# An SSM attention, a gated FFN and a second FFN on one core: a new prologue, attention visits in two parts, and new ranks

## The chip, the cores and the metric

The kernel runs on one core of a Trainium2 chip. The metric is the device time of one execution in microseconds, as the median of several runs. The core's engines run side by side, each through its own list of instructions in order: TensorE (PE, matmuls; PEld its weight loads), VectorE (DVE), ScalarE (ACT), GpSimd (POOL) and SyncE (SP), whose queue issues nearly all transfers. They wait for each other by semaphores.

## What is computed

Three stages, the output of one being the input of the next:

```python
# 1: for each of 4 x 8 heads, in chunks of the sequence (S = 768, D = 32, N = 16)
cum = np.cumsum(np.log(np.clip(a, 1e-06, 1.0))[chunk], axis=-1)
L = np.exp(cum[:, :, :, None] - cum[:, :, None, :]) * causal
y = einsum(C B^T * L, x) + einsum(C, state) * exp(cum)
state = exp(cum[last]) * state + einsum(B, x) * exp(cum[last] - cum)
# 2: FFN with a token shift, on y as [4 * 768, 256]
xk = mu_k * x + (1 - mu_k) * x_prev;  xr = mu_r * x + (1 - mu_r) * x_prev
k = np.maximum(xk @ w_k, 0.0);  v = k * k @ w_v             # 256 -> 1024 -> 256
x = v / (1.0 + np.exp(-(xr @ w_r)))
# 3: FFN, 256 -> 2048 -> 256
h = x @ w_in;  out = (h - np.tanh(h)) @ w_out
```

The weights come in float64 and are decoded on the core into a high and a low part; each FFN product is made of three matmuls (high by high, low weight by high, high weight by low).

## The kernel before

*Attention.* Time is cut into 12 groups of 256 tokens (`GT`), three for each of four batches; a group holds 8 heads and four chunks of 64 (`NC4`, `L`). For group k: `xb_load` and `bc_load` fetch the inputs; `rows` fetches the cumulated logarithms in a high and a low part (`sr`, `rr`) from `dcum`, a scratch in DRAM that the prologue writes; `decays` makes the differences of them on PE (`pd`), `decays_exp` their exponential on ACT (`L`); `scores` makes C B^T (`pcb`), `mask` multiplies it into `L` on DVE. `prep_rows` and `scales_sum`/`scales_exp` make exp(cum) for a batch (`pc`, `er`), `group_scale` multiplies it into C (`cp`), `weigh` multiplies B by its decay (`bp`), `chain` carries the state (`st`).

A *visit* k on PE is `scores(k+1)`, `inter(k)` (C by state), `terms(k+1)` (what group k+1 adds to the state) and `intra(k)` (masked scores by x), 32 + 32 + 16 + 32 small fp32 matmuls (fewer `inter` or `terms` at the ends of a batch). `group_out` copies the result into `xall`.

*First FFN*: 6 blocks of 512 tokens. `mix` and `mix_ahead` make the two inputs; they are split into `xh` and `xl`; then 8 products `up`, 2 `receptance`, and 8 `down_part`, of six 512-column matmuls each (`MM6`); between up and down a relu, a square and the split into `h` and `l`, on ACT or DVE; `final` ends a block. *Second FFN*: 6 blocks of 16 products up and 16 down, with a polynomial on ACT and DVE between.

*Weights*: `decode` fetches a block of 512 KB (`raw`) and works on it with one square on ACT and five operations on DVE (`wd`, `keep`, the low part `w..l`), the high part on either.

*Order.* The start is written out by hand: `START` names pieces of the prologue, and each engine gets its instructions in that order. `warm` is 14 matmuls on a tile of zeros. After it, `Plan.run` orders everything: a task has the engines that can run it, a time for each, what it comes after, ring buffers that it takes and uses, and a rank. At each step the planner takes the task that can start first by its own model of times, the lower rank first among those. `RANK_...` are constants that set the ranks, so a change of them moves instructions on all engines.

```python
START = """
    xl qz Da Dla Dca Db0 Dx0 mr warm ms rc sc mk seg cA lA cC cD lC lD hA rA f00 f01 tA xe las cum tri heads zk r1 Db1 Dx1 W f10 f11 pr0 Db2 Dnk Dnr
    p0 dec dexp d0 e0 ps pe w0 ob u0 d1 e1 w1 m0 h0 s0 r2 v0 o0 nu
""".split()
```

`hA` and `rA` are the first cumulated sums for groups 0 and 1 in `sr`, `tA` the same for `kl`; `f00`, `f01`, `f10`, `f11` copy rows of `sr` into `rr` by DMA (`first_rows`); `rc`, `sc`, `heads` write constants with `affine_select` on POOL; `cum` makes the sums of all groups and writes `dcum`; `W` fetches the first weight block; `p0` to `v0` are group 0 up to its visit.

Of the kernel before, what the change touches and what calls it, by code (L numbers as in the profile page):

```python
# [11 lines left out]
I32 = mybir.dt.int32  # L12
# [28 lines left out]
SPARE = 3.89  # L41
RANK_T = 9.83
RANK_F0, RANK_F, RANK_R, RANK_U, RANK_D = 28.81, 25.83, 10.39, 7.47, 14.62
RANK_G0, RANK_G, RANK_LAG = 313.17, 0.0, -1.88
RANK_W0, RANK_W = -2.86, 5.66
RANK_X0, RANK_X = -69.94, 9.75
RANK_E0, RANK_E = 64.82, 8.06
# [12 lines left out]
    xl qz Da Dla Dca Db0 Dx0 mr warm ms rc sc mk seg cA lA cC cD lC lD hA rA f00 f01 tA xe las cum tri heads zk r1 Db1 Dx1 W f10 f11 pr0 Db2 Dnk Dnr  # L60
    p0 dec dexp d0 e0 ps pe w0 ob u0 d1 e1 w1 m0 h0 s0 r2 v0 o0 nu
# [4 lines left out]
START_AT = dict(P=12.5, A=10.8, V=11.2, G=8.0, S=10.0)  # L66
# [40 lines left out]
class Plan:  # L107
# [3 lines left out]
    OVERLAP = dict(P=0.0, A=0.09, V=0.08, G=0.04, S=0.0)  # L111
    SEEN = dict(P=0.22, A=0.05, V=0.05, G=0.05, S=0.0)
# [82 lines left out]
def chain_kernel(ctx, tc, xb, a, an, a0, bc, mu_k, mu_r, w_k, w_v, w_r, w_in, w_out, out):  # L195
# [38 lines left out]
    dec = const.tile([P, NG, NC4, NQ], F32, name="dec")  # L234
# [38 lines left out]
    for _ in range(NE):  # L273
# [5 lines left out]
        pair=Ring(3, ("pd", 1), ("pcb", 1), ("py", 0)), xb=Ring(3, 0, 1), bc=Ring(3, 0, 1, 2), rows=Ring(3, 0, 1), L=Ring(2, 0, 1), bp=Ring(2, 0, 1), cp=Ring(2, 0),  # L279
# [82 lines left out]
    CUM, LOW, ROW, NR, TN = 64, 96, 112, 116, 72  # L362
    CQ = NC4 * NQ
    kls = [att.tile([TN, S], F32R, name=f"kl{i}") for i in range(2)]
    heads = att.tile([TN, 2, NQ, NS], F32R, name="heads")
    sr = att.tile([NR, 3, 2, L], F32R, name="sr")
    rr = att.tile([NR, 3, CQ, L], F32R, name="rr")
    dcum = dram.tile([2, NG, CQ, 2, L], F32, name="dcum")
# [13 lines left out]
    def apart(k):  # L382
        return bct[k][:, GT:].rearrange("p (c e i) -> p c e i", c=NC4, e=2)
# [15 lines left out]
    def scales_sum(b, lo=0, hi=S):  # L399

        if b not in er:
            er[b] = att.tile([P, S], F32, tag="er", bufs=2, name="er")
        pcv = pcs[b] = bank("pc").rearrange("p a b -> p (a b)")
        for o in range(lo, hi, BLK):
            e = min(hi, o + BLK)
            PE.matmul(pcv[:, o - lo:e - lo], heads.rearrange("p h q n -> p (h q n)"), kls[b % 2][:, o:e], start=True, stop=True)
# [33 lines left out]
    def weigh(k):  # L440
# [3 lines left out]
            in1=dec[:, k].unsqueeze(3).to_broadcast([P, NC4, NQ, NS]), op=ALU.mult,  # L444
# [99 lines left out]
    def prologue(fetch1):  # L544
# [5 lines left out]
        ad = t2[:LOW + CQ, 0, 0:GT]  # L550
# [532 lines left out]
```

## Time and profile before

| | |
|---|---|
| median of 3 runs | 526.59 us (525.16 to 528.76) |
| profiled execution | 527.53 us, of it 525.8 us span |
| PE busy | 484.5 us (92%) |
| DVE busy | 402.9 us (77%) |
| ACT busy | 289.5 us (55%) |
| POOL busy | 8.8 us (2%) |
| mean granted TensorE clock | 0.958 |
| DMA, mean | 52 GB/s |

The span runs from the first to the last instruction in the profile. An engine's busy time is the union of its instructions; what it waited for is in the views of waits. The granted clock is a share of full speed, 2.4 GHz; 0.50 is 1.2 GHz.

### The profile page before, as it was taken

The page shows a single profiled execution, that of the slowest core. Times are in us where ns is not written, and L with a number is a line of the kernel's source. Part 1 is how long each engine was busy: PE and PEld are TensorE (multiplying, and loading weights), DVE is VectorE, ACT ScalarE, POOL GpSimd, SP SyncE. Part 2 cuts the span into 40 slices and gives each one's busy share as a digit, 9 for nine tenths or more (in the row PEclk, how much of TensorE's full clock was granted, in tenths as well). Part 3 has the DMA queues.
Part 4 walks back from the last instruction along what each step waited for, and adds up shares of the span by engine and source line. Part 5 has one row for each costly group of instructions (what it writes and reads, how often), then busy time and mean ns, then how long its engine had stood idle before and what let it go on. Part 6 is the DMA issues. An engine that isn't in the chain of part 4 may idle for free.

```text
span 525.8 us, 10261 instructions
## 1 busy us (share of the span) xinstructions
PE 484.5 (92%) x4448; PEld 386.1 (73%) x4448; DVE 402.9 (77%) x511; ACT 289.5 (55%) x368; POOL 8.8 (2%) x19
## 2 busy tenths in 40 slices
PE   6557897989999999999999999999999999999994
PEld 3335676867787888777778878888878888887883
DVE  5487887777876899999787787687776966887682
ACT  3265684538383677665756455455554554465551
POOL 6000000000000000000000000000000000000000
PEclk8585999889999999999999999999999999999998
DMA  2766423233100323321000010010010001001001
GB/s 89 222 163 179 159 87 138 61 105 100 38 2 2 104 72 90 94 81 43 0 1 0 0 41 0 1 40 2 1 41 0 1 0 41 0 0 41 0 1 46
DMA packets 15403, 27.47 MB, mean 52 GB/s; under 512 B 3368, under 2 KB 4472, under 8 KB 15352
## 3 DMA queue, kind: packets, MB, share of 16 engines
q1 hardware_dynamic: 15352, 26.75, 16.4%
q8 instruction: 37, 0.61, 0.5%
q14 instruction: 14, 0.11, 0.1%
HBM read 23.37 MB, written 3.34 MB: 51 GB/s over the span
## 4 chain that ended last, share of the span: by engine, by line
PE 70%; DVE 11%; ACT 6%; DMA 6%; issue 4%; POOL 1%; SPq 1%; POOLq 0%; ACTq 0%; DVEq 0%
PE acc L743 10%; PE acc L745 10%; PE acc L744 10%; PE ph L733 8%; PE ph L736 8%; PE ph L734 8%; PE pk L733 3%; PE pk L734 3%; PE pk L736 3%; PE pcb L471 2%; PE py L503 2%; PE py L481 1%; DMA raw<-in_w_out 1%; DMA rr<-sr 1%; ACT h L351 1%
## 5 line engine op out<-in xcount | busy, mean ns | idle before, releaser
L862 ACT ACTIVATE s<-ph 128x1024 f32<-128x1024 f32 (+1 forms) x49 | 49.4, 1009 | 71.9 <-PE ph L736 71.9
L867 DVE SCALAR_TENSOR_TENSOR f<-f,s 128x1024 f32<-128x1024 f32 (+1 forms) x49 | 58.8, 1200 | 33.9 <-ACT f L863 33.6
L351 ACT ACTIVATE h<-f 128x1024 fp32r<-128x1024 f32 (+1 forms) x47 | 48.9, 1041 | 49.7 <-DVE f L871 45.8
L733 PE MATMUL ph<-xh,winh 128*128 128x512 f32 x192 | 75.6, 394 | 0.0
L734 PE MATMUL ph<-xh,winl 128*128 128x512 f32 x192 | 75.6, 394 | 0.0
L743 PE MATMUL acc<-h,wouth 128*128 128x512 f32 x188 | 74.5, 396 | 0.2
L745 PE MATMUL acc<-l,wouth 128*128 128x512 f32 x188 | 74.3, 395 | 0.1
L744 PE MATMUL acc<-h,woutl 128*128 128x512 f32 x188 | 73.9, 393 | 0.0
L880 DVE TENSOR_TENSOR l<-f,h 128x1024 fp32r<-128x1024 f32 (+1 forms) x49 | 58.9, 1201 | 18.6 <-ACT h L351 18.0
L871 DVE TENSOR_TENSOR f<-ph,f 128x1024 f32<-128x1024 f32 (+1 forms) x49 | 58.8, 1200 | 3.3
L736 PE MATMUL ph<-xl,winh 128*128 128x512 f32 x192 | 60.0, 394 | 0.0
L863 ACT ACTIVATE f<-s,biases 128x1024 f32<-128x1024 f32 (+1 forms) x49 | 55.6, 1135 | 1.6
L743 PEld LDWEIGHTS acc<-h,wouth 128*128 128x128 f32 x188 | 35.4, 188 | 9.6 <-ACT f L863 1.4
L734 PEld LDWEIGHTS ph<-xh,winl 128*128 128x128 f32 x192 | 36.2, 188 | 8.3
L736 PEld LDWEIGHTS ph<-xl,winh 128*128 128x128 f32 x192 | 36.1, 188 | 8.2
L733 PEld LDWEIGHTS ph<-xh,winh 128*128 128x128 f32 x192 | 36.1, 188 | 8.2
L745 PEld LDWEIGHTS acc<-l,wouth 128*128 128x128 f32 x188 | 35.4, 188 | 9.2 <-DVE l L880 0.9
L744 PEld LDWEIGHTS acc<-h,woutl 128*128 128x128 f32 x188 | 35.5, 189 | 8.0
L733 PE MATMUL pk<-xh,wkh 128*128 128x512 f32 x96 | 40.1, 418 | 0.8 <-DVE st L538 0.8
L734 PE MATMUL pk<-xh,wkl 128*128 128x512 f32 x96 | 39.1, 408 | 0.0
L743 PE MATMUL acc<-h,wvh 128*128 128x512 f32 x96 | 38.5, 401 | 0.2 <-DVE xall L795 0.2
L745 PE MATMUL acc<-l,wvh 128*128 128x512 f32 x96 | 38.0, 395 | 0.5 <-DVE l L766 0.5
(134 smaller groups left out, 753.8 us busy)
## 6 DMA issues: line engine op xcount, KB each, us to landing
bct<-in_bc SPq DMA_DIRECT2D x12, 384.0 KB
xbt<-in_xb SPq DMA_DIRECT2D x12, 384.0 KB
raw<-in_w_in SPq DMA_DIRECT2D x8, 512.0 KB
raw<-in_w_out SPq DMA_DIRECT2D x8, 512.0 KB
out<-ob SPq DMA_DIRECT2D x11, 256.0 KB
raw<-in_w_k SPq DMA_DIRECT2D x4, 512.0 KB
raw<-in_w_v SPq DMA_DIRECT2D x4, 512.0 KB
raw<-in_w_r SPq DMA_DIRECT2D x1, 512.0 KB
```

The costliest lines, as they stand in the source:

```text
L351: A.activation(out=out, in_=in_, func=AF.Copy)
L733: PE.matmul(o, wh[:, k, ms], hi[:, k], start=k == 0, stop=False)
L734: PE.matmul(o, wl[:, k, ms], hi[:, k], start=False, stop=False)
L736: PE.matmul(o, wh[:, k, ms], lo[:, k], start=False, stop=k == 1)
L743: PE.matmul(acc[:, c], wh[:, k, cs], h[:, e], start=first, stop=False, skip_group_check=True)
L744: PE.matmul(acc[:, c], wl[:, k, cs], h[:, e], start=False, stop=False, skip_group_check=True)
L745: PE.matmul(acc[:, c], wh[:, k, cs], l[:, e], start=False, stop=last, skip_group_check=True)
L862: A.activation(out=s, in_=phs[j, i][:, e], func=AF.Square, accum_out=sums[:, c:c + 1])
L863: A.activation(out=qs[j, i][:, e], in_=s, func=AF.Square, scale=PA, bias=pbias)
L867: V.scalar_tensor_tensor(out=q, in0=q, scalar=PG, in1=s, op0=ALU.add, op1=ALU.mult)
L871: V.tensor_tensor(out=q, in0=phs[j, i][:, e], in1=q, op=ALU.mult)
L880: V.tensor_tensor(out=l[:, e], in0=qs[j, i][:, e], in1=f(h[:, e]), op=ALU.subtract)
```

## The change

*Prologue.* The constants in `rr` are no longer made by selects on full tiles: POOL makes a small tile (`mk`, 64 + 16 columns) and DVE (group 0) and ACT (group 1) copy it with a broadcast into `rr`; `heads` likewise from 8 columns. High and low rows, which lay in separate bands of partitions, now lie in one band (`CUM` to `ROW`) and are made from one tile of 48 rows; two per-partition numbers (`sign`) choose the high or the low part. `first_rows` is one transfer per half of the heads instead of two; the one for group 0 is issued on ACT's queue. The loads of group 1 (`Db1`, `Dx1`) and the first weight block (`W`) are issued before the first sums. `rows` is two transfers instead of four, `prep_rows` one instead of two, in layouts that follow a new `dcum`; `sr` and `rr` have two buffers instead of three (`Ring(2, ...)`). `w1` stands behind `h0` and `s0`. `fa` and `fb` put 8 and 6 matmuls on zeros behind `u0` and behind visit 0. The first `er` is made from `sr`, not from `kl`.

*Visits.* `visit` is cut into `visit_a` (`scores`, `inter`) and `visit_b` (`terms`, `intra`). They are two tasks; between them stands a task of 1.5 us on a made-up engine X, which issues nothing. The mask of the next group comes after the first half, no longer after the whole visit.

*Layout.* Inside `L`, `cp` and the second part of `bct` the half (e) now stands ahead of the chunk (c); column counts don't change.

*Ranks.* All constants have new values.

```diff
-SPARE = 3.89
-RANK_T = 9.83
-RANK_F0, RANK_F, RANK_R, RANK_U, RANK_D = 28.81, 25.83, 10.39, 7.47, 14.62
-RANK_G0, RANK_G, RANK_LAG = 313.17, 0.0, -1.88
-RANK_W0, RANK_W = -2.86, 5.66
-RANK_X0, RANK_X = -69.94, 9.75
-RANK_E0, RANK_E = 64.82, 8.06
+SPARE = 18.01
+PAUSE = 1.5
+RANK_T = 8.09
+RANK_F0, RANK_F, RANK_R, RANK_U, RANK_D = 26.98, 22.7, 14.0, 7.19, 15.13
+RANK_G0, RANK_G, RANK_LAG = 188.07, 0.0, -5.09
+RANK_W0, RANK_W = 5.2, 6.85
+RANK_X0, RANK_X = 162.75, 0.58
+RANK_E0, RANK_E = 65.74, 11.53
...
-    xl qz Da Dla Dca Db0 Dx0 mr warm ms rc sc mk seg cA lA cC cD lC lD hA rA f00 f01 tA xe las cum tri heads zk r1 Db1 Dx1 W f10 f11 pr0 Db2 Dnk Dnr
-    p0 dec dexp d0 e0 ps pe w0 ob u0 d1 e1 w1 m0 h0 s0 r2 v0 o0 nu
+    mk pidx still xl qz Da Dla Db0 Dx0 Dca warm sign m0t m0b seg m1t cA lA cC lC Db1 Dx1 hA tri cD lD xe f0 W m1b f1 heads las cum spread zk pr0 Db2 Dnk Dnr
+    p0 dec dexp d0 e0 ps pe w0 ob u0 fa d1 e1 m0 h0 s0 w1 v0 fb o0 nu
...
     def rows(k):
-        for x, o in enumerate((CUM, LOW)):
-            nc.sync.dma_start(out=f(sr[o:o + CQ, k % 3]), in_=dcum[x, k])
-        for h2 in range(2):
-            o = ROW + 2 * h2
-            nc.sync.dma_start(out=f(rr[o:o + 2, k % 3]), in_=dcum[:, k, :, h2])
+        nc.sync.dma_start(out=f(sr[CUM:TOK, k % 2]), in_=dcum[k].rearrange("h x q c i -> (x q c) h i"))
+        nc.sync.dma_start(out=f(rr[ROW:NR, k % 2]), in_=dcum[k].rearrange("h x q c i -> (h x) (q c) i"))
 
     def prep_rows(b, lo=0):
-        for x in range(2):
-            d = dcum[x, NGB * b + lo // GT:NGB * (b + 1)].rearrange("g (c q) h i -> (q h) (g c) i", c=NC4)
-            nc.sync.dma_start(out=f(kls[b % 2][32 * x:32 * x + NH, lo:]), in_=d)
+        d = dcum[NGB * b + lo // GT:NGB * (b + 1)].rearrange("k h x q c i -> (h x q) k (c i)")
+        nc.sync.dma_start(out=f(kls[b % 2][TOK:ROW, lo:]), in_=d)
...
     def visit(k):
 
+        visit_a(k)
+        visit_b(k)
+
+    def visit_a(k):
         if k + 1 < NG:
             scores(k + 1)
         out_bank(k)
         inter(k)
+
+    def visit_b(k):
...
+        def t_mk():
+
+            G.memset(mk, 0.0)
+            select(mk[0:L, 0:L], [[1, L]], 0, -1, ALU.is_ge, -32768.0)
+            for x in range(2):
+                select(mk[CUM:TOK, L:], [[1, CQ]], CQ * x, -1, ALU.not_equal, -1.0)
+
+        def moving(k, top, e):
+            if top:
+                o, i = rr[0:L, k].rearrange("p q c i -> p (q c) i"), mk[0:L, 0:L].unsqueeze(1).to_broadcast([L, CQ, L])
+            else:
+                o, i = rr[CUM:ROW, k].rearrange("p q c i -> p (q c) i"), mk[CUM:ROW, L:].unsqueeze(2).to_broadcast([ROW - CUM, CQ, L])
+            return lambda: copy(e, o, i)
...
+            o = sr[CUM:ROW].rearrange("p k h j -> p (k h j)")
+            V.tensor_tensor_scan(out=ad, data0=seg[CUM:ROW], data1=ad, initial=0.0, op0=ALU.mult, op1=ALU.add)
+            V.tensor_copy(o, ad)
+            V.tensor_scalar(out=ad, in0=ad, scalar1=sign[CUM:ROW, 0:1], scalar2=None, op0=ALU.mult)
+            V.scalar_tensor_tensor(out=o, in0=f(o), scalar=sign[CUM:ROW, 1:2], in1=ad, op0=ALU.mult, op1=ALU.add)
+
+        def first_rows(k, e):
             def fn():
                 for h2 in range(2):
-                    r = ROW + 2 * h2 + x
-                    o = (CUM, LOW)[x]
-                    nc.sync.dma_start(out=f(rr[r:r + 1, k]), in_=f(sr[o:o + CQ, k, h2]))
+                    r = ROW + 2 * h2
+                    e.dma_start(out=f(rr[r:r + 2, k]), in_=f(sr[CUM:TOK, k, h2]))
...
-                rw = put(dict(S=1.3), lambda e, k=k: rows(k), [], at(k - 1.2), [(R["rows"], k)], dma=0.2)
+                rw = put(dict(S=0.9), lambda e, k=k: rows(k), [], at(k - 1.2), [(R["rows"], k)], dma=0.2)
...
-                uses = [(R["L"], j), (R["xb"], j), (R["cp"], j), (R["state"], j), (R["bp"], k), (R["xb"], k), (R["bc"], k)]
-                need = [MK[j], CH[j], GS[j], XL.get(j), XL.get(k), BL.get(k), BPt.get(k), D.get(k), PS.get(b) if k < NG else None]
-                visited = put(dict(P=2.3 if k < NG else 1.1), lambda e, j=j: visit(j), need, at(j), take, uses)
+                use_a = [(R["cp"], j), (R["state"], j), (R["bc"], k)]
+                use_b = [(R["pair"], ("py", j)), (R["L"], j), (R["xb"], j), (R["bp"], k), (R["xb"], k)]
+                first_half = put(dict(P=1.85 if k < NG else 0.85), lambda e, j=j: visit_a(j), [CH[j], GS[j], BL.get(k), D.get(k), PS.get(b) if k < NG else None, MK[j]], at(j), take, use_a)
+                pause = put(dict(X=PAUSE), lambda e: None, [first_half])
+                visited = put(dict(P=1.25 if k < NG else 0.75), lambda e, j=j: visit_b(j), [pause, XL.get(j), XL.get(k), BPt.get(k)], at(j), (), use_b)
...
-            MK[k] = put(dict(V=t_dve(1024)), lambda e, k=k: mask(k), [visited, E.get(k)], at(k), (), [(R["pair"], ("pcb", k)), (R["L"], k)])
+            MK[k] = put(dict(V=t_dve(1024)), lambda e, k=k: mask(k), [first_half, E.get(k)], at(k), (), [(R["pair"], ("pcb", k)), (R["L"], k)])
```

Three places, as the programs list them. SP at the start (`raw<-in_w_k` is `W`, `rr<-sr` are the first rows), before:

```order
L557 DMA s<-in_a 112x256
L557 DMA f<-in_a 128x192
L557 DMA f<-in_an 96x256
L380 DMA bct<-in_bc 128x768
L376 DMA xbt<-in_xb 128x768
L622 DMA rr<-sr 1x16x64 x4
L629 DMA dcum<-l 96x2x256
```

and in the changed kernel:

```order
L565 DMA s<-in_a 48x256
L565 DMA f<-in_a 128x192
L381 DMA bct<-in_bc 128x768
L377 DMA xbt<-in_xb 128x768
L565 DMA f<-in_an 96x256
L381 DMA bct<-in_bc 128x768
L377 DMA xbt<-in_xb 128x768
L303 DMA raw<-in_w_k 128x2x512
L645 DMA rr<-sr 2x16x64 x2
L653 DMA dcum<-l 24x4x256 x2
```

The loads of group 1 and the first weights now stand ahead of the rows and of `dcum`; before they stood behind both. DVE in group 0's turn of the prologue, from the decay weights `bp` on, before:

```order
L442 TENSOR_TENSOR bp<-xbt,dec 128x256 x2
L521 TENSOR_TENSOR L<-pcb,L 128x512 x2
L535 COPY st<-py 128x64
L538 SCALAR_TENSOR_TENSOR st<-st,er,py 128x64 x3
L418 TENSOR_TENSOR cp<-bct,er 128x512
```

and in the changed kernel:

```order
L443 TENSOR_TENSOR bp<-xbt,dec 128x256
L528 TENSOR_TENSOR L<-pcb,L 128x512 x2
L542 COPY st<-py 128x64
L545 SCALAR_TENSOR_TENSOR st<-st,er,py 128x64 x3
L419 TENSOR_TENSOR cp<-bct,er 128x512
L443 TENSOR_TENSOR bp<-xbt,dec 128x256
```

`weigh(1)`, the second `bp`, stood ahead of the mask and stands behind `cp`. PE in visit 5 (`pcb` scores, `py<-cp` inter, `py<-xbt,bp` terms, `py<-L` intra, `acc` a down product, `pc` the sums of a batch), before:

```order
L471 MATMUL pcb<-bct 32x128 x32
L481 MATMUL py<-cp,st 32x64 x32
L496 MATMUL py<-xbt,bp 32x64 x16
L503 MATMUL py<-L,xbt 32x64 x32
L733 MATMUL pk<-xh,wkh 128x512
```

and in the changed kernel:

```order
L472 MATMUL pcb<-bct 32x2x64 x32
L482 MATMUL py<-cp,st 32x64 x32
L765 MATMUL acc<-h,wvh 128x512
L766 MATMUL acc<-h,wvl 128x512
L767 MATMUL acc<-l,wvh 128x512
...
L407 MATMUL pc<-kl_109,heads 128x512
L407 MATMUL pc<-kl_109,heads 128x256
L497 MATMUL py<-xbt,bp 32x64 x16
L504 MATMUL py<-L,xbt 32x64 x32
```

A product of six matmuls (three of them shown) and the sums stand between `inter` and `terms`, where before nothing did.

## Rows read from the trace of the kernel before

**Rows 1.** Busy time by stage; mean clock, DMA share and GB/s at the end.

```profile
0.00:50.60 50.60, 30.01 (x776) 19.13 (x777) 32.23 (x73) 22.89 (x37) 8.85 (x19) 0.70 0.55 161
57.00:101.00 44.00, 37.35 (x761) 30.17 (x746) 35.19 (x59) 29.28 (x36) 0.00 (x0) 0.96 0.36 117
101.00:180.00 79.00, 73.64 (x1438) 59.85 (x1438) 60.47 (x89) 45.17 (x54) 0.00 (x0) 0.98 0.18 55
180.00:515.00 335.00, 333.89 (x1438) 269.31 (x1436) 268.33 (x279) 189.63 (x240) 0.00 (x0) 1.00 0.08 24
20.00:253.00 233.00, 209.11 (x3191) 167.61 (x3191) 194.01 (x302) 142.97 (x176) 0.12 (x1) 0.93 0.30 91
```

**Rows 2.** PE's waits from 50.6 to 180: us in total, times, longest.

```profile
PE py L503 <- issue: 9.3, 6, 3.2
PE py L496 <- issue: 1.2, 1, 1.2
PE py L481 <- ACT f L783: 1.0, 1, 1.0
...
```

**Rows 3.** Busy time and counts between the ends of two such waits.

```profile
76.68:91.71 15.03, 11.88 (x253) 9.72 (x254) 12.07 (x19) 7.07 (x9) 0.00 (x0) 1.00 0.38 126
111.33:127.33 16.00, 15.08 (x254) 11.96 (x254) 13.47 (x22) 7.35 (x7) 0.00 (x0) 0.89 0.28 87
```

**Rows 4.** The page: busy engines with instruction counts; a DMA queue.

```profile
PE 484.5 (92%) x4448; PEld 386.1 (73%) x4448; DVE 402.9 (77%) x511; ACT 289.5 (55%) x368; POOL 8.8 (2%) x19
...
q8 instruction: 37, 0.61, 0.5%
```

**Rows 5.** Busy time and clock (third from the end) after two long waits.

```profile
92.20:95.60 3.40, 3.40 (x14) 2.60 (x10) 2.36 (x6) 1.73 (x3) 0.00 (x0) 0.50 0.52 143
112.70:116.10 3.40, 3.40 (x10) 2.63 (x9) 3.29 (x8) 0.00 (x0) 0.00 (x0) 0.50 0.74 211
```

**Rows 6.** Timeline of the prologue: start, us, engine, line, operation [idle before].

```profile
1.09 6.04 PE L554 MATMUL acc<-quiet 128*128 128x512 bf16 x14 [1.09 <-DVE quiet L658]
...
12.31 1.22 PE L427 MATMUL pd<-rr,sr 116*128 116x512 f32 x2 [1.11 <-DMA rr<-sr]
...
13.95 2.42 SPq L622 DMA_DIRECT2D rr<-sr  x4
...
14.71 1.08 PE L496 MATMUL py<-xbt,bp 64*32 64x64 f32 x32 [0.96 <-ACT L L438]
...
18.52 0.42 DVE L442 TENSOR_TENSOR bp<-xbt,dec 128x256 f32<-128x256 f32 x1 [4.44 <-DMA xbt<-in_xb]
18.86 1.28 DVE L521 TENSOR_TENSOR L<-pcb,L 128x512 f32<-128x512 f32 x2
...
21.03 1.20 PE L427 MATMUL pd<-rr,sr 116*128 116x512 f32 x2 [5.24 <-DMA rr<-sr]
...
21.21 0.69 DVE L418 TENSOR_TENSOR cp<-bct,er 128x512 f32<-128x512 f32 x1
...
25.97 1.27 PE L503 MATMUL py<-L,xbt 64*32 64x64 f32 x59
```

**Rows 7.** Timeline of DVE from 28 us on, and PE's first FFN matmul.

```profile
28.94 1.23 DVE L538 SCALAR_TENSOR_TENSOR st<-st,er,py 128x64 f32<-128x64 f32 x4 [2.11 <-ACT er L409]
...
31.29 0.42 DVE L313 TENSOR_SCALAR wd<-raw 128x512 uint32<-128x512 uint32 x1
31.62 0.68 DVE L328 TENSOR_TENSOR wkl<-keep,wkh 128x512 fp32r<-128x512 f32 x1
32.23 0.68 DVE L316 SCALAR_TENSOR_TENSOR wd<-raw,wd 128x512 uint32<-128x512 uint32 x1
...
38.38 1.22 DVE L521 TENSOR_TENSOR L<-pcb,L 128x1024 f32<-128x1024 f32 x1
...
45.24 1.22 DVE L766 TENSOR_TENSOR xl<-f,xh 128x1024 fp32r<-128x1024 f32 x1
...
50.63 0.77 PE L733 MATMUL pk<-xh,wkh 128*128 128x512 f32 x1 [0.83 <-DVE st L538]
```

More of the change, by code (lines that the diff above doesn't have):

```diff
@@ L357, in select @@
         G.affine_select(out=t, in_=f(t), pattern=pattern, base=base, channel_multiplier=cm, compare_op=op, fill=fill)
-    CUM, LOW, ROW, NR, TN = 64, 96, 112, 116, 72
+    CUM, TOK, ROW, NR = 64, 96, 112, 116
     CQ = NC4 * NQ
[L364 to L368, printed above, removed]
+    kls = [att.tile([ROW, S], F32R, name=f"kl{i}") for i in range(2)]
+    heads = att.tile([NR, 2, NQ, NS], F32R, name="heads")
+    sr = att.tile([NR, 2, 2, L], F32R, name="sr")
+    rr = att.tile([NR, 2, NQ, NC4, L], F32R, name="rr")
+    dcum = dram.tile([NG, 2, 2, NQ, NC4, L], F32, name="dcum")
     NC = NB * NH * S // GT
@@ L403, in scales_sum @@
         pcv = pcs[b] = bank("pc").rearrange("p a b -> p (a b)")
+        hv = heads.rearrange("p h q n -> p (h q n)")
+        if hi == GT:
+            PE.matmul(pcv[:, 0:GT], hv, sr.rearrange("p k h j -> p (k h j)"), start=True, stop=True)
+            return
         for o in range(lo, hi, BLK):
             e = min(hi, o + BLK)
-            PE.matmul(pcv[:, o - lo:e - lo], heads.rearrange("p h q n -> p (h q n)"), kls[b % 2][:, o:e], start=True, stop=True)
+            PE.matmul(pcv[:, o - lo:e - lo], hv[0:ROW], kls[b % 2][:, o:e], start=True, stop=True)
     def scales_exp(b, lo=0, hi=S):
@@ L415, in group_scale @@
     def group_scale(k):
-        cp[k] = att.tile([P, NC4, 2, L], F32, tag="cp", bufs=2, name="cp")
-        by = scale(k).rearrange("p (c i) -> p c i", c=NC4).unsqueeze(2).to_broadcast([P, NC4, 2, L])
-        V.tensor_tensor(out=cp[k], in0=apart(k), in1=by, op=ALU.mult)
+        cp[k] = att.tile([P, 2, NC4 * L], F32, tag="cp", bufs=2, name="cp")
+        by = scale(k).unsqueeze(1).to_broadcast([P, 2, NC4 * L])
+        V.tensor_tensor(out=cp[k], in0=bct[k][:, GT:].rearrange("p (e t) -> p e t", e=2), in1=by, op=ALU.mult)
     pds = {}
@@ L423, in decays @@
         pd = pds[k] = bank("pd")
-        mt[k] = att.tile([P, 2, NC4, 2, L], F32, tag="L", bufs=2, name="L")
+        mt[k] = att.tile([P, 2, 2, NC4, L], F32, tag="L", bufs=2, name="L")
         for g in range(2):
-            by = rr[:, k % 3].rearrange("p (c q) i -> p c (q i)", c=NC4)[:, :, 2 * L * g:2 * L * (g + 1)]
-            PE.matmul(pd[:, g], sr[:, k % 3].rearrange("p h j -> p (h j)"), by, start=True, stop=True)
+            by = rr[:, k % 2, 2 * g:2 * g + 2].rearrange("p q c i -> p (q c i)")
+            PE.matmul(pd[:, g], sr[:, k % 2].rearrange("p h j -> p (h j)"), by, start=True, stop=True)
     def flat(k):
-        return mt[k].rearrange("p g c e i -> p g (c e i)")
+        return mt[k].rearrange("p g e c i -> p g (e c i)")
     def parts(split):
@@ L470, in scores @@
                     r = quarter(q)
-                    PE.matmul(pcb[quarter(2 * h2 + jh), hp, t], bct[k][r, o:o + 32], bct[k][r, GT:][:, t], start=c == 0, stop=c == NC4 - 1, skip_group_check=True)
+                    PE.matmul(pv[quarter(2 * h2 + jh), hp, :, c], bct[k][r, o:o + 32], apart(k)[r, :, c], start=c == 0, stop=c == NC4 - 1, skip_group_check=True)
     def out_bank(k):
@@ L628, in t_cum @@
             V.tensor_tensor(out=cf[:, 1], in0=ca, in1=f(cf[:, 0]), op=ALU.subtract)
-            nc.sync.dma_start(out=dcum.rearrange("x g c h i -> x (g c h i)").rearrange("x (p s) -> p x s", s=GT), in_=f(cf))
+            for x in range(2):
+                nc.sync.dma_start(out=dcum[:, :, x].rearrange("k h q c i -> (k h) q (c i)"), in_=f(cf[:, x]))
         def t_las():
@@ L649, in t_nu @@
             G.memset(xall[:, :, 0:NB * (S + 1)].rearrange("p c (b s) -> p c b s", b=NB)[..., 0:1], 0.0)
-        def more(k):
-            return lambda: A.activation(out=rr[:, k], in_=f(rr[:, 0]), func=AF.Copy)
         def dummy(func):
@@ L1053, in columns @@
         return np.ascontiguousarray(channels(v).reshape(2, P).T)
-    heads = a.reshape(NB, NQ, 2, NGB, NC4, L).transpose(0, 3, 4, 1, 2, 5)
-    sums = np.ascontiguousarray(heads).reshape(NG, NC4 * NQ, 2 * L)
-    two = sums[0:2].transpose(1, 0, 2).reshape(NC4 * NQ, 2 * P)
+    heads = a.reshape(NB, NQ, 2, NGB, NC4, L).transpose(0, 3, 2, 1, 4, 5)
+    two = heads[0, 0:2].transpose(2, 3, 0, 1, 4).reshape(NC4 * NQ, 2 * P)
+    one = heads[0, 0].reshape(2, NQ, GT)
     def f64(v):
@@ L1063 @@
         "xb": np.concatenate([tokens(x), tokens(B)], axis=3),
-        "a": np.ascontiguousarray(heads.transpose(4, 5, 0, 1, 2, 3)).reshape(P, NG * NC4 * NQ),
-        "an": sums.reshape(-1, GT),
-        "a0": np.concatenate([np.tile(a[0, :, 0:GT], (8, 1)), two, two, two]),
+        "a": np.ascontiguousarray(heads.transpose(2, 5, 0, 1, 3, 4)).reshape(P, NG * NC4 * NQ),
+        "an": np.ascontiguousarray(heads).reshape(-1, GT),
+        "a0": np.concatenate([two, two, one[0], one[0], one[1], one[1]]),
         "bc": np.concatenate([states(B), apart(C)], axis=2),
```

88 lines of the change are left out of this document (41 added, 47 removed).

## The prediction

> **What bounds the kernel now.** I read the busy time by stage first [rows 1]. From 180 to 515 us TensorE (PE) is busy 333.9 of 335 us at full clock: the second FFN and the last blocks of the first are bound by PE, and their matmuls don't change. The time that an edit can win lies ahead of that. In the first 50.6 us PE is busy for 30.0, at a mean granted clock of 0.70; from 57 to 101 it is idle for 6.7 us, from 101 to 180 for 5.4.
>
> Then I read what PE waited for after its first FFN matmul [rows 2]. Two entries of 9.3 and 1.2 us stand at the attention matmuls of `intra` and `terms` under "issue": seven waits, for which no semaphore is shown. Third, the count of PE instructions between the ends of such waits [rows 3]: 254 matmuls and 253 weight loads, then 253 and 254, the same 507 each time whatever FFN work lies between. The page has a DMA queue of the kind "instruction" with 37 packets and 0.61 MB [rows 4], 16.5 KB each; PE's 8,896 matmuls and weight loads over 37 make 240 for each, about half of 507. I read these waits as PE running out of its own instruction stream: the 112 matmuls of a visit are some 450 short instructions for 3 to 4 us, those of an FFN product of 1.38 us only 12.
>
> Fourth, the clock after the two longest waits [rows 5]: the one of 3.2 us is followed by 3.4 us at 0.50 of full speed, which is 1.2 GHz, and the one of 2.2 us before 111.35 by another 3.4.
>
> Last, the opening [rows 6]. The `rr<-sr` transfers for group 1 are issued at 13.95, after two group loads and a weight block, and `decays(1)` starts at 21.03, 5.24 us late. VectorE (DVE) stands 4.44 us before `weigh(1)`, whose data come in the same batch, and the mask of group 0, which stands behind it, starts at 18.86, though its exponential was done when it released `terms(0)` at 14.71.
>
> **The change part by part.** The sum is made against the profiled execution, 527.53 us with a span of 525.8; it lies 0.9 over the median of 526.59. I take three terms and a charge.
>
> *Term A, the opening.* Removed: the selects over 1024 columns on GpSimd, two memsets, one of two sets of row transfers. Added: two DVE copies of 1024 columns, five tiny DVE operations, four passes over 48x256, one ACT copy more, and a wait of the first `rr<-sr` on ACT behind the third logarithm and a table load. No row shows a spread copy from a small tile; it lies between an operation on 512 columns, 0.68, and the mask on 1024, 1.22 [rows 7]. Both are below the selects, but ACT's order now holds the transfer. I take `decays(0)`, and the exponential with it, to stay where they are, with bounds of 1.3 us earlier and 1.7 later (a copy of 1.22 more and half a microsecond of issue). Group 1 and the first weights are issued right at the start, so `decays(1)` and `weigh(1)` find their data; `weigh(1)` now stands behind the mask and the state chain.
>
> So from 14.7 on DVE takes mask, chain and `cp` in the 3.04 us that they took from 18.86 to 21.90 [rows 6], and is done near 17.7. On PE `terms(0)` ends at 15.8 and the eight new fills come next: at the 0.43 us of the warm-up matmuls [rows 6] 3.4 us, to 19.2. They lie beside the DVE work, except for 1.5 us. Then `decays(1)` to `intra(0)`: 6.2 us as from 21.03 to 27.24 at half the clock, or down to 3.1 at the full one. They end between 22.3 and 25.4 against 27.24; I take 23.5, since PE has no gap left between 12.3 and there. Six more fills cost 1.3 to 2.6 us. From the end of `intra(0)` to the state chain of group 1 it took 1.7 us, to 28.94 [rows 7]: now it starts near 23.5 + 1.3 + 1.7 = 26.5.
>
> From there DVE sets the pace up to `xl`, the last factor of the first FFN input. In the new order 23 rows stand from that chain to `xl`. In a packed stretch DVE starts the next operation 0.6 us after one on 512 columns (31.62 to 32.23), 0.33 after a short one and 1.2 after one on 1024 [rows 7]: 16.4 us in all. That gives 42.9 for the end of `xl`, which was at 46.46. The first four matmuls of a product don't need `xl`, so PE starts the first product near 42, where it started at 50.63, after visit 2 in both: 8.6 us. By then it will also have done `decays(4)`, `scores(4)` and `inter(3)`, 2.2 us of work that came later. Term A is 10.8 us; with all bounds against it 8, with all for it 13.
>
> *Term B, the visit in two parts.* `visit_b` is ranked apart, with a pause of 1.5 us that occupies no engine. In the new PE order the visits 3, 4 and 6 to 11 have two products between `inter` and what follows, 2.76 us; visit 5 has one and the sums' two matmuls, about 1.7, and visits 1 and 2 have only the sums. These products are work that PE had to do anyway, so they cost nothing where their inputs are ready; the cover is DVE and ACT being ahead with the mixes and squares. The six waits in `intra` lasted 0.76 to 3.16 and the one in `terms` 1.2 [rows 2]. With 2.76 us between, a wait of 3.16 leaves 0.4; with 1.7 it leaves up to 1.5. Of 10.5 I take 9.5; the bounds are 6 (half of the blocks end elsewhere in the visit, where nothing stands between) and 10.5.
>
> The Trainium skill, page "Runtime: NRT & Kernel Launch", section "Instruction fetch mechanics", says that an engine's instructions come in blocks of 16 KiB and that crossing into the next is "mostly hidden". The block size agrees with the 16.5 KB of [rows 4], the hiding does not agree with the 10.5 us. By that sentence the stall would have another cause, terms B and C would be nothing, and the gain 12.9 us smaller; this is the second rival.
>
> *Term C, the clock.* Two stretches of 3.4 us at 0.50 follow waits of 3.16 and 2.18 us [rows 5]. Half of each is lost, 1.7 us, 3.4 in all. Where no such wait is left, neither is the fall. The slow start of the first FFN (50.6 to 54.7, 2.0 us) I leave as it is, because PE is idle for half of the 10 us before it in the new order too. Bounds 0 and 5.4.
>
> *The charge, new waits.* The new ranks let four visits run before the first FFN block and put products where the planner's model has their inputs ready. Two places look tight to me: the first down product needs `l`, which stands 13 DVE rows or 10 us behind `xl`, while PE reaches it 9 us after its first product, some 2 us early; and the second `wv` block is due within 1 us of its use. I charge 4 us, with bounds of 0 (the largest wait on another engine between 50.6 and 180 was 1.0 [rows 2]) and 8.
>
> Row buffers go from three to two: `rows(k)` is issued after `decays(k-2)`, two visits earlier, and four issues become two. Cost nothing unless the transfer lands later than that; this is the third rival. Stacking halves and heads differently changes no column count of a matmul or of a DVE operation.
>
> Sum: 10.8 + 9.5 + 3.4 - 4 = 19.7. 527.5 - 19.7 = 507.8 for the profiled execution, and 0.9 less for the median: **507**. All bounds one way give 8 + 6 + 0 - 8 = 6, the other way 13 + 10.5 + 5.4 = 29.
>
> **The rivals.** *DVE becomes the bound.* Between 20 and 253 us DVE was busy for 194.0 [rows 1]. By the counts of the two orders it gives ACT copies worth 3.6 us, net: 190. With my forecast these have to fit in 213 us, 89%; it was 80% from 57 to 101 and 77% from 101 to 180 (35.19 of 44, 60.47 of 79). Where it can't be packed beyond 84%, the first FFN ends at 20 + 226 = 246, a gain of 7 to 8 us: 519. For: a long stretch where weights, masks and squares all wait for one engine. Against: much of DVE's idle time followed PE's own waits, and goes with them.
>
> *The split does nothing.* If the issue waits have another cause, or move to another place in the visit, terms B and C fall away: 10.8 - 4 = 6.8, 520. For: the pause is the planner's alone, PE isn't made to wait for anything. Against: the constant count of 507 [rows 3].
>
> *Slower, by the row buffers.* `decays(k)` stands ahead of `scores` on PE, in order, and its rows are queued on SyncE behind the group load and weight blocks. If they land late, all of PE waits: the worst seen is 5.24 us [rows 6]. At ten visits the gain of 19.7 is gone from 2 us a visit on, and at 3.5 us the time is 526.6 + 15 = 542. Against: after the third visit 10 us and more lie between one visit and the next, and in the trace no later `decays` waited for rows.
>
> **How the numbers follow.** Forecast (a gain of 13 to 28) 0.65; DVE bound 0.18; split without effect 0.09; slower 0.05; the rest, 0.03, a gain over 28. The range leaves out the slower case, the upper part of the two weak ones and the best end: 499 to 518. A measurement of this kernel can tell about 1%, 5.3 us, from no change. Faster by more: 0.65 + 0.03 and most of the two middle cases, 0.9. Within 1%: 0.05. Slower by more: 0.05.
>
> **What would show it.** The first FFN product near 42; `decays(1)` no longer waiting for `rr<-sr`; the mask of group 0 near 15. In the visits after it, "issue" at `intra` and `terms` under 2 us in total, and no fall of the clock between 60 and 180. New waits of PE on DVE `l` or `xl`, or on a weight, would be the charge; DVE busy for over 90% from 40 to 100 with PE waiting for it, the first rival. The end of the first FFN (the last `final`, before 253) should move to about 233, and the rest of the program should only shift. Wrong I would be above all if PE's new products stand and wait where the old order had work.

## The result, and the profile after

The changed kernel takes 505.6 us, median of 4 runs (505.0 to 507.4), against 526.9 before (4 runs, 525.2 to 528.8): a ratio of 0.960, 95% interval 0.956 to 0.964, 21.3 us. The profiled execution took 507.4 us, with a span of 505.7; it is the slowest of the four, with a mean clock of 0.978 where the others have 0.984 to 0.986, so the trace shows a little more half clock than they have.

The windows of the changed kernel, as those of [rows 1]; the columns are busy time with the number of instructions of PE, PEld, DVE, ACT, POOL, then the clock, the DMA share and GB/s:

```profile
0.00:20.00 20.00, 13.90 (x141) 6.48 (x149) 12.48 (x37) 8.13 (x15) 6.01 (x21) 0.83 0.60 184
20.00:42.80 22.80, 18.23 (x777) 13.55 (x761) 19.59 (x37) 15.71 (x24) 0.11 (x1) 0.85 0.72 219
42.80:100.00 57.20, 54.69 (x1138) 43.70 (x1128) 53.35 (x90) 43.06 (x54) 0.00 (x0) 0.97 0.45 138
100.00:180.00 80.00, 79.77 (x1075) 64.66 (x1074) 70.28 (x99) 53.76 (x64) 0.00 (x0) 1.00 0.18 53
180.00:505.70 325.70, 315.86 (x1361) 253.86 (x1360) 245.73 (x250) 172.45 (x219) 0.00 (x0) 0.99 0.06 20
20.00:230.00 210.00, 201.56 (x3190) 161.68 (x3175) 188.76 (x285) 144.15 (x180) 0.11 (x1) 0.98 0.32 97
```

From 42.8 to 180 us PE is now idle for 2.7 us in all. The last row is the answer to the first rival: DVE is busy for 188.8 of 210 us, 90%, and PE hardly waits for it. The waits of PE in that stretch, beside [rows 2]:

```profile
PE py L482 <- issue: 2.1, 1, 2.1
PE py L482 <- ACT f L805: 0.4, 1, 0.4
PE py L482 <- DVE f L807: 0.2, 1, 0.2
```

Seven issue waits of 10.5 us at `intra` and `terms` have become one of 2.1 us, at `inter` (L482 now). Ahead of 42.8 us there is another one, of 2.43 us, at `scores(3)` (33.82 in the timeline below); the prediction has no such wait. The opening in the timeline, beside [rows 6] and [rows 7] (start, duration, engine, line; in brackets the idle time before, and what ended it):

```profile
8.99 1.31 ACTq L645 DMA_DIRECT2D rr<-sr  x1
...
12.46 0.90 PE L428 MATMUL pd<-rr,sr 116*128 116x512 f32 x2 [2.60 <-DMA rr<-sr]
...
14.02 1.29 DVE L528 TENSOR_TENSOR L<-pcb,L 128x512 f32<-128x512 f32 x2 [0.95 <-ACT L L439]
...
15.54 3.59 PE L217 MATMUL acc<-quiet 128*128 128x512 bf16 x8
...
18.57 1.31 PE L428 MATMUL pd<-rr,sr 116*128 116x512 f32 x2
...
25.00 1.23 DVE L545 SCALAR_TENSOR_TENSOR st<-st,er,py 128x64 f32<-128x64 f32 x4 [0.34 <-ACT er L410]
...
33.82 0.47 PE L472 MATMUL pcb<-bct 32*32 32x128 f32 x8 [2.43 <-issue]
...
41.56 1.22 DVE L788 TENSOR_TENSOR xl<-f,xh 128x1024 fp32r<-128x1024 f32 x1
...
42.84 0.50 PE L755 MATMUL pk<-xh,wkh 128*128 128x512 f32 x1
...
230.06 1.22 DVE L817 TENSOR_TENSOR xall<-acc,s 128x1024 f32<-128x1024 f32 x1 [3.42 <-PE acc L767]
```

`decays(1)` starts at 18.57 with no wait for `rr<-sr`, the first FFN product at 42.84 instead of 50.63, and the last `final` at 230.06 instead of 252.06. Ahead of 180 us the clock stands at 0.50, which is 1.2 GHz, in three stretches: 12.8 to 19.6, and (windows as above)

```profile
74.20:77.60 3.40, 3.40 (x10) 2.62 (x9) 3.40 (x7) 1.58 (x2) 0.00 (x0) 0.51 0.83 266
33.30:40.10 6.80, 6.23 (x190) 4.69 (x190) 5.42 (x9) 6.80 (x11) 0.00 (x0) 0.50 0.79 251
```

The first of these follows the issue wait that ended at 73.60; the second sets in during the one that ended at 33.82. Before, such stretches made 41.0 us in all, now 17.0.

The span is PE's busy time plus its idle time, so the 20.1 us can be booked without a remainder: idle time fell from 41.3 to 23.2 us (7.9 less ahead of 45 us, 6.2 less from 45 to 100, 5.1 less from 100 to 180, and 1.1 more after 180), busy time from 484.5 to 482.5, in spite of 14 fills.

### The profile page after: what moved, and what is told of

Read it like the earlier page. It is cut to its first block, busy times and chain, and to the rows that moved or that the text cites. A ratio compares the mean times of both kernels' runs of the same rounds, so it can differ in the third digit from the quotient of the medians.

```text
span 505.7 us, 10270 instructions
## 1 busy us (share of the span) xinstructions
PE 482.5 (95%) x4462; PEld 382.3 (76%) x4462; DVE 401.4 (79%) x509; ACT 293.1 (58%) x374; POOL 6.1 (1%) x22
## 4 chain that ended last, share of the span: by engine, by line
PE 69%; DVE 18%; ACT 6%; DMA 3%; issue 2%; ACTq 0%; POOL 0%; DVEq 0%; POOLq 0%; SPq 0%
PE acc L765 10%; PE acc L767 10%; PE acc L766 10%; PE ph L755 8%; PE ph L758 8%; PE ph L756 8%; PE pk L755 3%; PE pk L756 2%; PE pk L758 2%; DVE l L788 2%; DVE f L889 2%; DVE f L893 1%; DMA raw<-in_w_in 1%; PE py L504 1%; PE py L482 1%
## 5 line engine op out<-in xcount | busy, mean ns | idle before, releaser
L902 DVE TENSOR_TENSOR l<-f,h 128x1024 fp32r<-128x1024 f32 (+1 forms) x49 | 58.9, 1201 | 18.6 <-ACT h L352 18.0
L352 ACT ACTIVATE h<-f 128x1024 fp32r<-128x1024 f32 (+1 forms) x43 | 44.7, 1039 | 48.5 <-DVE f L893 45.6
```

Of the source, the lines that this page charges most:

```text
L352: A.activation(out=out, in_=in_, func=AF.Copy)
L902: V.tensor_tensor(out=l[:, e], in0=qs[j, i][:, e], in1=f(h[:, e]), op=ALU.subtract)
```

## The experiments

My theory: TensorE runs out of its own instructions where short matmuls stand in a row, and the split gives it long ones in between (terms B and C); the opening gives a gain of its own (term A). The first rival to be tried is that the split does nothing. The table holds the medians, and from the profiled executions PE's idle time in four stretches, its busy time and the sum of its issue waits from 0 to 182 us. The intervals are 0.3 to 1.3% wide, so two kernels whose medians lie less than some 2 us apart aren't told from each other.

| kernel | us | ratio to before, 95% | idle 0-45 | 45-100 | 100-180 | 180-end | busy | issue |
|---|---|---|---|---|---|---|---|---|
| before | 526.9 | | 18.6 | 8.7 | 5.4 | 8.7 | 484.5 | 11.7 |
| changed | 505.6 | 0.956-0.964 | 10.7 | 2.5 | 0.2 | 9.8 | 482.5 | 4.7 |
| nosplit | 523.3 | 0.991-0.997 | 12.2 | 9.2 | 4.9 | 10.9 | 485.4 | 12.1 |
| split | 521.3 | 0.987-0.993 | 16.3 | 5.2 | 0.9 | 12.4 | 483.4 | 2.1 |
| prologue | 525.1 | 0.993-0.998 | 15.9 | 8.0 | 5.3 | 11.1 | 483.0 | 12.3 |
| shift | 515.8 | 0.975-0.984 | 18.7 | 2.8 | 1.2 | 9.2 | 481.8 | 3.4 |
| oldranks | 516.8 | 0.979-0.983 | 12.6 | 3.5 | 1.3 | 12.7 | 486.5 | 2.6 |
| three | 509.8 | 0.966-0.969 | 10.4 | 2.5 | 0.0 | 11.2 | 484.5 | 1.6 |
| pause0 | 517.1 | 0.979-0.988 | 13.3 | 7.5 | 0.3 | 11.2 | 482.8 | 9.2 |
| nofill | 503.9 | 0.953-0.966 | 12.9 | 1.5 | 0.2 | 9.9 | 478.4 | 5.1 |
| split_newranks | 510.1 | 0.962-0.972 | 18.1 | 4.5 | 0.2 | 9.0 | 477.2 | 6.4 |
| nosplit_shift | 513.0 | 0.970-0.978 | 12.4 | 5.7 | 0.5 | 11.2 | 485.4 | 5.5 |
| nofill_shift | 505.6 | 0.956-0.963 | 11.0 | 0.7 | 0.4 | 10.2 | 482.7 | 6.5 |
| prologue_shift | 519.4 | 0.983-0.993 | 17.6 | 3.1 | 2.6 | 11.1 | 483.7 | 8.0 |

**nosplit: the visit in one piece again.** The two halves and the pause become the one task of before, and `mask` comes after it:

```diff
-                pause = put(dict(X=PAUSE), lambda e: None, [first_half])
-                visited = put(dict(P=1.25 if k < NG else 0.75), lambda e, j=j: visit_b(j), [pause, XL.get(j), XL.get(k), BPt.get(k)], at(j), (), use_b)
+                visited = put(dict(P=2.3 if k < NG else 1.1), lambda e, j=j: visit(j), need, at(j), take, uses)
```

> The changed kernel with each visit as one piece again; new opening and new ranks stay. If TensorE ran out of its own instruction stream and the split covers that (terms B and C), issue waits of 1 to 3 us come back inside the visits, 8 to 13 us in all with the clock falls behind them: 514 to 518 us. If the split does nothing (second rival): 505.6, within 1%.

Measured 523.3 us, above the range: 17.7 of the 21.3 us are gone. The waits of PE from 42 to 180 us, and three of them in the timeline:

```profile
PE py L504 <- issue: 10.4, 6, 2.4
PE py L482 <- ACT L L439: 2.0, 3, 1.1
PE acc L765 <- issue: 0.8, 1, 0.8
```

```profile
58.63 0.31 PE L504 MATMUL py<-L,xbt 64*32 64x64 f32 x5 [1.88 <-issue]
...
76.48 0.42 PE L504 MATMUL py<-L,xbt 64*32 64x64 f32 x21 [2.37 <-issue]
...
88.36 0.39 PE L765 MATMUL acc<-l,wvh 128*128 128x512 f32 x1 [0.78 <-issue]
```

The waits are back, with the same size as before, and one of them stands at an FFN product, which no theory on `intra` explains. The rival that the split does nothing is refuted.

**split and prologue: one part alone on the kernel before.** The first has the halves, the pause and nothing else; the second the new opening, the one-piece visit and the old `RANK_` block.

> The kernel before with nothing but the visit in two parts with the pause of 1.5 us; old opening and old ranks. Terms B and C alone: 526.9 - 12.9 = 514 us, no issue wait at the matmuls of intra and terms beyond 2 us in total after 57 us, no clock at 0.50 between 60 and 180. If the split does nothing: 527. If it needs the new ranks, because the old ones leave no product ready between the two parts: 520 to 524, with issue waits left.

> The changed kernel with the visit as one piece and the old ranks: the new opening alone. Term A: 526.9 - 10.8 = 516 us, the first FFN product 8 us earlier than 50.6, and the waits of 10.5 us in the visits still there. If what the opening wins is lost again behind it (VectorE or the weights set the pace): 521 to 527.

Measured 521.3 and 525.1 us. The split takes away what it was meant to (issue 2.1 us instead of 11.7), but 3.7 us of idle time came up after 180 us, and the first FFN block waits for its inputs. So the time is that of the third case, but not for its reason: issue waits are not what is left. The opening alone brings 1.9 us, not 10.8, though its first FFN product starts at 39.84, earlier than in the changed kernel; but 564 matmuls of the trace stand ahead of that product, where 776 did before: a visit has only gone behind it. PE's waits from 0 to 182 us in it:

```profile
PE py L497 <- issue: 6.3, 4, 2.0
PE py L504 <- issue: 6.0, 4, 2.3
PE pk L753 <- ACT xh L352: 4.1, 1, 4.1
PE pc L407 <- DMA kl<-dcum: 2.8, 1, 2.8
```

Time won at the start is spent on waits for `xh` and `kl`, and the issue waits are untouched (12.3 us). A first product that starts early was the wrong measure of term A, unless the same work stands ahead of it.

**shift: the boundary, by itself.** The kernel before, with two of 14 warm-up matmuls replaced by 56 tiny ones, which take 1.56 us. Nothing else changes in any engine's list; the first scores start at 6.50 instead of 7.06, and every later PE instruction stands 108 places further on.

```diff
+            for _ in range(56):
+                PE.matmul(acc[0:32, 0, 0:32], quiet[0:32, 0:32], quiet[0:32, 0:32], start=True, stop=True)
...
-warm=lambda: warm(14)
+warm=lambda: warm(12)
```

> The kernel before, with 56 matmuls of 32 x 32 in place of two of the 14 warm-up matmuls: 108 TensorE instructions more ahead of everything, about the same time, no other change. If a wait stands at every 256th TensorE instruction and costs what TensorE is faster than 3.05 us for 256 instructions, the boundaries move by 108 instructions; with the times of the trace of before, without its waits, the sum of waits between 28 and 180 us falls from 8.8 (by the same sum at no shift) to 4 us, and with up to two clock falls fewer the time is 517 to 523. If the waits belong to intra (its operands, its place in the visit, the clock), they stay where they are: 527.

Measured 515.8 us, 11.2 faster than before, for instructions that do nothing; that is a little more than the best that was expected, 517. PE's waits from 50.6 to 180 us, the first of the list and the two under issue:

```profile
PE pk L735 <- DVE st L538: 0.8, 1, 0.8
...
PE acc L745 <- issue: 0.6, 1, 0.6
...
PE py L503 <- issue: 0.2, 1, 0.2
```

10.5 us at `intra` and `terms` became 0.2, with 0.6 more at an FFN product. In the sums, issue fell by 8.3 us, and busy time by 2.7 (the clock is 0.91 from 45 to 100 us and 1.00 from 100 to 180, where it was 0.88 and 0.98). The same instructions with the same operands in the same order don't wait: what decides is their number in PE's stream. In all 14 traces I counted the matmuls, weight loads and semaphore instructions of PE up to and with the matmul that ends each issue wait of 0.7 us or more between 20 and 182 us. All 50 stand at 194 plus a multiple of 256. The Trainium skill, page "Runtime: NRT & Kernel Launch", section "Instruction fetch mechanics", gives 256 instructions for a block; these 50 waits agree with that number. Its "mostly hidden" holds from 180 us on, where 256 instructions take some 30 us and no boundary shows a wait.

**pause0: halves without a pause.** `PAUSE = 0.0` in the changed kernel.

> The changed kernel with a pause of 0: in the order of TensorE one product of 1.38 us then stands between inter and terms in most visits and none in one, instead of two. If 256 instructions need 3.05 us and a visit takes some 1.8, one product is nearly enough: 505 to 508 us, issue waits within 1.5 us of the changed kernel's. If two are needed: 509 to 513.

Measured 517.1 us; one product isn't enough, and the expectation was wrong. Three of its waits:

```profile
37.88 0.81 PE L504 MATMUL py<-L,xbt 64*32 64x64 f32 x59 [3.08 <-issue]
...
52.03 0.60 PE L504 MATMUL py<-L,xbt 64*32 64x64 f32 x36 [1.16 <-issue]
...
61.86 0.35 PE L504 MATMUL py<-L,xbt 64*32 64x64 f32 x17 [1.54 <-issue]
```

My 3.05 us for 256 instructions, the least distance of two boundaries with a wait at the second in the trace of before, was too short for this stretch: in the three waits above the next block's instruction packet (see the last section) started 2.3 to 2.4 us after PE entered the block before it, beside data transfers that kept the DMA engines 80 to 88% busy; in the two waits of before from which the 3.05 was taken it started after 0.6 and 0.7 us, with the engines idle or nearly so. The pause is worth 11.5 us, 4.5 of them issue.

**three: a pause between scores and inter too.** `visit_a` is cut into `scores` and a task for `inter`, with another pause before it.

> The changed kernel with the visit in three parts, a pause of 1.5 us also between scores and inter, so that products can stand at both places. If the wait of 2.1 us left in inter at 71 us and the half clock of 3.4 us behind it come from 256 instructions in a row that are faster than their fetching: both go, 501 to 504 us. If that wait has another cause, or the extra pieces bring new waits for the score banks: 505 to 510.

Measured 509.8 us. The wait in `inter` and the half clock behind it are gone (issue 1.6 instead of 4.7, clock 1.00 from 45 to 100), so its cause was the same. But the time is at the upper end of what was expected if that wait had another cause, and in PE's waits from 0 to 182 us stand new ones:

```profile
PE pc L407 <- DMA kl<-dcum: 2.5, 1, 2.5
...
PE acc L771 <- DVE wvl L329: 0.8, 1, 0.8
PE acc L770 <- ACT wvh L352: 0.7, 1, 0.7
PE pk L760 <- ACT wkh L352: 0.7, 1, 0.7
PE pk L760 <- ACT xh L352: 0.6, 1, 0.6
```

Products put between the pieces come earlier than their weights. This is the charge of the prediction, in another order. In all PE's idle time is 24.0 us against 23.2 in the changed kernel, so the waits have only changed their place, and its busy time is 2.0 us longer.

**oldranks and split_newranks: the ranks and the opening, each left out.** The first is the changed kernel with the old `RANK_` block and `SPARE`, the second the kernel before with the split and the new block.

> The changed kernel with the old ranks: new opening and split, without the third part. If opening and split carry the gain and the ranks only trade waits (the charge): 504 to 508 us. If the opening's gain needs the new ranks (alone, with the old ranks, it gave 1.9 us and left waits of 4.1 us for xh and 2.8 us for kl before the first FFN products): 510 to 516, with these waits there again.

> The kernel before with the split and the new ranks, on the old opening: all of the change but its first part. If the opening is worth term A (7 us of idle TensorE ahead of 45 us and some 3 us at half clock), 513 to 517 us. If it is worth what it gave alone, 1.9 us: 506 to 509.

Measured 516.8 and 510.1 us; the first is just above what was expected with the ranks needed (510 to 516), the second in neither of its ranges. With the split in place the parts add up: the opening brings 4.5 us with the old ranks (521.3 to 516.8) and 4.5 with the new (510.1 to 505.6), the ranks 11.2 on either opening (521.3 to 510.1, 516.8 to 505.6). Without the split the ranks bring 1.8 (525.1 to 523.3). So the ranks are half of the gain, and, as far as was tried, only behind the split. It isn't gained at the issue waits: with the old ranks these are shorter, 2.6 us against 4.7. The opening can be seen by itself in the first FFN product, ahead of which split_newranks and the changed kernel do the same work (888 matmuls in the trace, and the 14 fills): it starts at 47.95 there and at 42.84 here, 5.1 us earlier.

```profile
47.95 0.50 PE L742 MATMUL pk<-xh,wkh 128*128 128x512 f32 x1
```

With the old ranks, PE's waits from 0 to 182 us hold

```profile
PE pc L407 <- DMA kl<-dcum: 2.7, 1, 2.7
...
PE acc L767 <- DVE l L788: 2.5, 2, 2.1
```

and 12.7 us of idle time after 180; busy time is 4.1 us longer, with a clock of 0.71 instead of 0.86 from 20 to 45 us. How much of the 4.1 belongs to the ranks is open: this execution has a mean clock of 0.966, the other three of the same kernel 0.976 to 0.979. Which of the constants brings the gain, and by what, was not tried.

**nosplit_shift and prologue_shift: padding in place of the split.** The edit of shift with 90 and with 50 tiny matmuls.

> The changed kernel with the visit in one piece, and 90 matmuls of 32 x 32 in place of two warm-up matmuls: 176 TensorE instructions more at the start. By the times of the kernel in one piece without its waits, and 3.05 us for 256 instructions, the waits between 20 and 182 us fall from 8.1 to 3.6 us. If the split only covers these waits, padding does part of its work: 515 to 519 us, against 523.3 without the padding. If the split is worth what it is for another reason: 521 to 525.

> The new opening alone (old ranks, visit in one piece) with 50 matmuls of 32 x 32 in place of two warm-up matmuls: 96 TensorE instructions more at the start; by the same sum the waits fall from 10.6 to 4.3 us. If the boundaries moved against the new opening and hid its gain: 510 to 516 us. If the opening is worth 1.9 us with the old ranks whatever the boundaries do: 517 to 520 at best, by the waits alone. If the waits don't follow the boundaries: 525.

Measured 513.0 us, better than the 515 to 519 expected, and 519.4. Padding does 10.3 of the split's 17.7 us, and leaves 5.5 us of issue waits, near the 4.7 of the changed kernel; the rest, 7.4, is what the split does beside it (`inter` waits for `L` 3.2 us in one piece, and 0.8 in the changed kernel). Under the old ranks the opening with padding, 519.4, stays behind the old opening with padding, 515.8. This comparison isn't clean, since the first still has 8.0 us of issue waits (4.3 were expected) and the second 3.4. With these taken off, 511.4 and 512.4 are left: the boundaries hid some of the opening's gain, but with the old ranks what is left is 1 us, and 2.4 by the same sum without padding.

**nofill and nofill_shift: without the 14 fills, and then with 114 tiny matmuls.**

> The changed kernel without the 14 fill matmuls of the opening. If they lie in gaps of TensorE and only hold up its clock: 506 to 509 us, the clock at 0.50 for longer before 42 us. If they stand in the way of the opening: 503 to 505, the first FFN product before 42.

> The changed kernel without the 14 fills, and 114 matmuls of 32 x 32 in place of two warm-up matmuls: 224 TensorE instructions more at the start. By the same sum as before no wait is left (without the padding 0.9, measured 5.1 under issue). If the waits left ahead of 35 us depend on where the boundaries fall: 499 to 502 us. If not, as without the fills: 503 to 505.

Measured 503.9 (503.3 to 509.6, 4 runs) and 505.6 us; the second lies in neither of its ranges. The fills are 4.1 us of busy time, and without them the clock from 45 to 100 us is 1.00, not 0.97, but the intervals of the three kernels overlap: no version shown faster than the changed kernel came out. The padding did not remove the waits ahead of 42 us:

```profile
29.64 1.12 PE L504 MATMUL py<-L,xbt 64*32 64x64 f32 x57 [1.54 <-issue]
...
34.70 0.82 PE L482 MATMUL py<-cp,st 32*32 32x64 f32 x60 [0.97 <-issue]
...
40.18 0.68 PE L504 MATMUL py<-L,xbt 64*32 64x64 f32 x31 [3.19 <-issue]
```

Here four visits follow each other with few products between, about two boundaries in each, and wherever a boundary falls there is short work on both sides.

## Why the prediction was right, step by step

507 was predicted and 505.6 measured, 19.7 and 21.3 us of gain; the terms met it less well than the sum.

*Term A* (10.8): as the trace shows it, the first product moved by 7.8 us instead of 8.6, with `decays(4)`, `scores(4)` and `inter(3)` ahead of it as foreseen; PE's idle time ahead of 45 us fell by 7.9. But of these three only the last two came later before; `decays(4)` already stood ahead of the first product, at 50.63:

```profile
48.57 1.23 PE L427 MATMUL pd<-rr,sr 116*128 116x512 f32 x2
...
56.81 1.15 PE L471 MATMUL pcb<-bct 32*32 32x128 f32 x64
58.94 0.72 PE L481 MATMUL py<-cp,st 32*32 32x64 f32 x48 [0.98 <-ACT f L783]
```

So the work that moved is 1.9 us, not the 2.2 of the prediction, and the term comes to 9.7. The single steps came near: mask at 14.02 (near 15), `intra(0)` done at 22.7 (22.3 to 25.4), state chain at 25.00 (26.5), `xl` done at 42.78 (42.9). What was wrong is whose gain it is. I booked it to the new opening; that part is worth 4.5 us behind the split, with either ranks, and 1.9 by itself, so nothing like 10.8 in any of the three places where it was measured. The rest needs the new ranks, for which I had only a charge.

*Term B* (9.5): 10.5 us of issue waits became 2.1, a gain of 8.4. The wait left stands at `inter`, the case that my lower bound named. The cause, a count of instructions, is shown by shift. The some 450 instructions of a visit hold: the trace lists each of its 112 small matmuls twice (`pcb` x64 where the program has x32), so they are 224 matmuls and 224 weight loads, 448. One detail was wrong: what I counted between two waits, 507 and, read rightly, 508 [rows 3], are two blocks of 256 with their semaphore instructions, of which only the second boundary waited. And the wait of 2.4 us at `scores(3)`, ahead of the stretch that I summed, is in no term.

*Term C* (3.4): one of the two stretches of 3.4 us at half clock is gone, 1.7 us; the other follows the wait left. The 2.0 us at the start of the first FFN, which I had left as they were, came on top, since the half clock now ends at 40.1: 3.7 in all.

*The charge* (4): 0.6 us of waits on other engines from 42.8 to 180. `l` and the second `wv` block came in time. The charge was taken too high here, and what the new ranks bring, 11.2 us behind the split, is not in the prediction at all. oldranks and three show that such waits are real where the order is another.

7.8 and 1.9, 8.4, 3.7 and no charge make 21.8, against 20.1 in the spans; 1.1 of the difference is the idle time after 180 us, the rest I can't assign.

That the sum came so near is in part luck. By the parts of the change, put in one after the other, the split brings 5.7 us, the ranks 11.2 and the opening 4.5; the prediction has 12.9 for the split, a loss of 4 for the ranks and 10.8 for the opening. The split and the opening were taken too high by 13.5 us together, the ranks too low by 15.2.

*The rivals.* DVE at 90% is not the bound: PE waits for it for 0.2 us from 42.8 to 180. The split does nothing: refuted by nosplit and split. Row buffers: no `decays` after the opening waits for its rows.

## What to carry to other kernels

Where an engine waits and no semaphore is shown, count its instructions between the ends of such waits; if the counts are multiples of one number, pad the stream at its start with tiny instructions, and see whether the waits move. Short instructions in a row are then a cost by themselves, and the cure is long work between them, placed by the order, not a faster chain. Parts of a change that share an engine must be measured on top of each other: here the split was worth 5.7 us alone and 17.7 us behind the other two, and with the opening alone the first FFN product started 11 us earlier, with a visit less ahead of it, for a gain of 1.9.

## What the runs showed of the hardware

The packets of the instruction queue (q8) can be laid beside the waits. Each of the 50 waits counted above ends 2.2 to 3.0 us after the start of the packet that came while PE was in the block before; where one packet came and there was no issue wait of 0.2 us or more, PE reached the boundary 2.2 us or more after it in 188 of 194 cases from 20 to 182 us. I read that packet as what PE waits for. PE can be short of instructions with no other transfer at all. In the kernel before it entered a block at 136.43 and waited at the next one's boundary; from 136.43 to 139.47 the queues moved this alone, and it started at 137.05:

```profile
139.47 0.77 PE L503 MATMUL py<-L,xbt 64*32 64x64 f32 x56 [1.04 <-issue]
```

```profile
q8 instruction: 1, 0.02, 1.8%
```

Beside data transfers the packet tends to come later. The wait of 2.1 us left in the changed kernel ended at 73.60, at PE instruction 3266. PE had entered the block before at instruction 3010, 67.54 us. The DMA queues from 67.54 to 71.25, and then from 71.25 to 71.60 (packets, MB, share of the 16 engines):

```profile
q1 hardware_dynamic: 455, 1.03, 85.3%
```

```profile
q1 hardware_dynamic: 52, 0.12, 88.8%
q8 instruction: 1, 0.02, 17.2%
```

So the instruction packet comes 3.7 us or more after PE entered the block, and until then the data queue kept the engines 85% busy. PE entered another block at 42.19; from 42.20 to 43.30 the engines were 8% busy, and the packet came behind that, 1.1 to 1.3 us after the entry (the queues from 42.20 to 43.30, then to 43.50):

```profile
q1 hardware_dynamic: 35, 0.03, 8.1%
```

```profile
q8 instruction: 1, 0.02, 29.5%
```

In that case PE met no wait at the next boundary. Over the 14 traces, from 20 to 182 us, the packet came 0.9 us after the entry (median of 126 blocks) where the other queues kept the engines under 10% busy until then, and 1.9 us (median of 52) where they kept them over 80% busy; single blocks go from 0.5 to 4.4 us in the second group, and from 0.1 to 5.2 in the first. That the transfers cause the delay is read from this; no run changed the transfers alone. The second thing that I had not expected is the size: 56 matmuls without any use made a tuned kernel 2% faster.
